# Earlier loads of the first weights, and a 128-token item turned in mid-chunk, in a fused attention, mixture-of-experts and SwiGLU kernel

## The chip, the cores and the metric

The kernel runs on one core of a Trainium2 chip. The metric is the device time of one execution, in microseconds (us); the median of three runs is given. TensorE is called PE here, VectorE DVE, ScalarE ACT, GpSimd POOL and SyncE SP, as the profile does.

## What is computed

Block-sparse attention (2 batches, 8 heads, 768 positions, 64 per head) gives 1536 tokens of 512 numbers. Each token goes to the one expert of eight that a gate picks, then through a dense SwiGLU layer. Cut to what matters:

```python
x = attention(q, k, v)                                   # 1536 x 512
logits = x @ w_gate + modality_bias[modality_id]
e_idx = np.argmax(logits, axis=1)
gate_w = softmax(logits)[arange(N), e_idx]
for e in range(8):
    mask = e_idx == e
    h = np.maximum(x[mask] @ w1[e], 0.0)                 # 512 -> 1024
    out[mask] = gate_w[mask, None] * (h @ w2[e])         # 1024 -> 512
x = out
return (silu(x @ w_g) * (x @ w_v)) @ w_o                 # 512 -> 1536 -> 512
```

## The kernel before

**Stages.** Attention runs over 24 units of 128 tokens and four heads (`st_s`, `st_e`, `st_t`, `st_v`). A finished block of 128 tokens is stored to the scratch tensor `x_d` (L728), turned (`st_x`, L349) and multiplied with the gate matrix (`st_l`, L360). Routing (`route`, `route_early`, `route_where`, `route_items`) builds index tables on DVE with small matmuls on PE. The experts' work is cut into items, `KIND = "TQQSP"`: item 0 has 384 tokens of the fullest expert, chosen from the first 768 tokens alone, items 1 and 2 have 512 tokens, item 3 has 128 and item 4 has 256. The SwiGLU layer follows.

**Two floats for one.** Every product is three matmuls (`mm3`, L820 to L822): high by high, low by high, high by low. So tokens and weights are split into a high part, which ACT writes, and a low part, which DVE writes: `xh` and `xl` of the tokens (L770, L771), `wh` and `wl` of a weight chunk (L801, L802), `hh` and `hl` of the hidden layer (L839, L842), `yh` and `yl` of the result (L874, L875).

**An item.** Its tokens are gathered from `x_d` into `xs` by indirect DMAs on POOL's queue (`gather`, L748, 128 rows each), scaled by the gate weight on DVE (`scale_x`, L755), and turned on PE with their split (`split_x`, L768 to L771; for the 128-token item `split_x1`, L792 to L794). For 384 tokens `split_x` has four parts of three transposes, which use the PSUM banks V, P, V, P in turn. There are two V banks and one P bank, so the fourth part waits until DVE has read the second. Then come four chunks of the hidden layer (`hidden`, 24 matmuls each, in two halves with a bank T each) and four chunks of the projection (`project`, 24 matmuls each), and `store_y` moves the result out of PSUM.

**Weights.** A chunk is 512 KB. SP reads the expert's number from the table `tab` into a register (L936) and issues the chunk's DMA into one of three `raw` buffers (`load_w`, L816). `load_to(n)` issues the loads up to the n-th, `split_to(n)` splits chunks up to the n-th and issues loads that far ahead that three are under way. The chunks' order is the list `preps`; `take` hands out a split chunk and has the one three places further split.

**What sets the order.** The program is written out in the order in which each engine is to work (a manual schedule); every engine runs its instructions in that order and waits on semaphores. Two places matter here.

The first is the change from attention to item 0, here the first seam. `route_early` finds the fullest expert (L450 writes `tab`), forms the index of its tokens, gathers them and then loads three chunks:

```python
first_x.append(gather(pl["xg"], *idx_of(0), rows=128 * b))    # L468
load_to(RB)                                                   # L469, RB = 3
```

Further down come the scaling (L1092), the split of the first chunk (L1094) and the split of the tokens (L1100), then item 0's hidden layer (L1115).

The second is the change from item 1's projection to item 2's hidden layer, here the second seam. Item 3's 128 tokens are scaled and turned between the two:

```python
    bg_step(STEPS["Q"])      # L1308, after each of four projected chunks
scale_x(xs)                  # L1318, after the fourth
x1 = split_of(3, xs)         # L1319
```

`bg_step` runs pieces of a list in the background: the decoding of the SwiGLU weights from 64-bit floats (L1237 to L1258) and the routing tables for the output rows. `sorted_tokens` (L1194 to L1200) is called after the third projected chunk: 24 small matmuls, and a copy of their result by DVE (L1200).

Of the kernel before, what the change touches and what calls it, by code (L numbers as in the profile page):

```python
# [7 lines left out]
F32 = mybir.dt.float32  # L8
# [4 lines left out]
ALU = mybir.AluOpType  # L13
# [6 lines left out]
def sparse_attention_moe_swiglu_kernel(  # L20
# [18 lines left out]
    nc = tc.nc  # L39
# [41 lines left out]
    NC1 = FF // 256  # L81
# [351 lines left out]
    def route_early():  # L433

        b = GROUPS[0][1]
        c0 = cnt[:, 0]
        TB_ = BLOCKS["T"]
        w = w_p.tile([128, 6, E], F32, tag="r_ew", bufs=1, name="r_ew")
        m8, fs, n0 = w[:, 0, 0:1], w[:, 0, 1:2], w[:, 0, 2:3]
        nc.vector.tensor_reduce(out=m8, in_=c0, op=ALU.max, axis=AX.X)  # L440
        yield
        nc.vector.scalar_tensor_tensor(out=w[:, 1], in0=c0, scalar=m8, in1=wts, op0=ALU.is_equal, op1=ALU.mult)
        nc.vector.tensor_scalar(out=n0, in0=m8, scalar1=-1.0, scalar2=float(-CT), op0=ALU.mult, op1=ALU.max)
        nc.vector.tensor_scalar(out=sc[0][:, 16:17], in0=m8, scalar1=float(CT), scalar2=None, op0=ALU.min)
        yield
        nc.vector.tensor_reduce(out=fs, in_=w[:, 1], op=ALU.max, axis=AX.X)
        yield
        nc.vector.scalar_tensor_tensor(out=w[:, 2, 0:TB_], in0=fs.to_broadcast([128, TB_]), scalar=-16.0,
                                       in1=kc[:, 0, 0:TB_], op0=ALU.mult, op1=ALU.add)
        nc.vector.tensor_scalar(out=tab[:, 0, 0:1], in0=fs, scalar1=-1.0, scalar2=float(E), op0=ALU.mult, op1=ALU.add)  # L450
        nc.vector.tensor_scalar(out=w[:, 3], in0=wts, scalar1=fs, scalar2=None, op0=ALU.is_equal)
        yield
        TB = [128, b, TB_]
        nc.vector.tensor_tensor(out=bo[:, 0:b, 0:TB_], in0=w[:, 2, 0:TB_].unsqueeze(1).to_broadcast(TB),
                                in1=code[:, 0:b].unsqueeze(2).to_broadcast(TB), op=ALU.is_equal)
        nc.vector.scalar_tensor_tensor(out=cnt[:, 2], in0=w[:, 3], scalar=n0, in1=c0, op0=ALU.mult, op1=ALU.add)
        nc.vector.tensor_scalar(out=w[:, 4:6].rearrange("p a e -> p (a e)")[:, 0:b], in0=fm_r[:, 0:b], scalar1=fs,
                                scalar2=-float(TB_), op0=ALU.is_equal, op1=ALU.mult)
        yield True
        ip = bank("T")  # L460
        for t in range(b):
            for j in range(2):
                nc.tensor.matmul(out=ip[:, 0:TB_], lhsT=a1[0, j][:, t, :], rhs=bo[:, t, 0:TB_],
                                 start=(t == 0 and j == 0), stop=(t == b - 1 and j == 1))
        nc.vector.tensor_copy(out=idx[:, 0:TB_], in_=ip[:, 0:TB_])
        nc.vector.tensor_tensor(out=code[:, 0:b], in0=code[:, 0:b],
                                in1=w[:, 4:6].rearrange("p a e -> p (a e)")[:, 0:b], op=ALU.add)
        first_x.append(gather(pl["xg"], *idx_of(0), rows=128 * b))  # L468
        load_to(RB)  # L469
        yield  # L470

    first_x = []
# [258 lines left out]
    pl = {}  # L731


    RB, WB = 3, 3
# [18 lines left out]
    def scale_x(xs):  # L753
        for t in xs:
            nc.vector.tensor_scalar(out=t[:, 0:DM], in0=t[:, 0:DM], scalar1=t[:, DM:DM + 1], scalar2=None, op0=ALU.mult)  # L755
# [38 lines left out]
        nc.vector.tensor_tensor(out=xl, in0=p, in1=xh.bitcast(F32), op=ALU.subtract)  # L794
        return xh, xl

    def split_w(pool, src, eng, tags=("wh", "wl")):
        a, b = src.shape[1], src.shape[2]
        wh = pool.tile([128, a, b], F32R, tag=tags[0], name="wh")
        wl = pool.tile([128, a, b], F32R, tag=tags[1], name="wl")  # L800
        nc.scalar.activation(out=wh, in_=src, func=ACTF.Copy)  # L801
        eng.tensor_tensor(out=wl, in0=src, in1=wh.bitcast(F32), op=ALU.subtract)  # L802
        return wh, wl

    def load_w(pool, e, which, c):
# [46 lines left out]
    def project(c, hs, w, yp, cols=(0, 1), between=None):  # L852
        for k in range(4):
            if k == 2 and between is not None:
                between()
            kk = 4 * (c % 2) + k
            h = hs[kk // 2]
            for dd in cols:
                sl = slice(128 * dd, 128 * dd + 128)
                own = len(yp) == 1 and len(cols) == 2  # L860
                y = yp[0][:, dd] if own else yp[dd][:, 0]
                mm3(y, w[0][:, k, sl], w[1][:, k, sl], h[0][:, kk % 2, :], h[1][:, kk % 2, :],
                    kk == 0 and (dd == 0 or not own), kk == 2 * NC1 - 1 and (dd == 1 or not own))
# [53 lines left out]
    for j in range(NS):  # L917
# [3 lines left out]
        if j == JS - 1:  # L921

            one = [(wn, JS, c) for c in range(NC1) for wn in ("w1", "rows")]
# [3 lines left out]
    ready = {}  # L927
# [4 lines left out]
    def load_to(n):  # L932
        while n_load[0] < min(n, len(preps)):
            wn, j, c = preps[n_load[0]]
            if j not in e_reg:
                e_reg[j] = nc.sync.value_load(tab[0:1, 0, j:j + 1], min_val=0, max_val=E - 1)  # L936
            loaded[wn, j, c] = load_w(pl["raw"], e_reg[j], wn, c)
            n_load[0] += 1

    def split_to(n, limit=None):  # L940
        limit = len(preps) if limit is None else limit
        while n_split[0] < min(n, limit):
            key = preps[n_split[0]]
            load_to(min(n_split[0] + RB, limit))
            ready[key] = split_w(pl["wc"], loaded.pop(key), nc.vector)
            n_split[0] += 1
        load_to(min(n_split[0] + RB, limit))

# [3 lines left out]
    def split_of(j, xs, tags="VP", later=None):  # L952
        if KIND[j] == "S":
            return split_x1(pl["s1"], xs)
        return split_x(pl["xg"], xs, tags, later)
# [135 lines left out]
    st_x(NT - 2)  # L1091
    scale_x(first_x[0])  # L1092
    st_v(NM - 1)
    split_to(1, 2 * NC1)  # L1094
    heads.close()
    open_h()

    while rg:
        adv(1000)
    x = split_of(0, first_x[0])  # L1100
    st_z(NT - 2)
    st_x(NT - 1)
    split_to(2, 2 * NC1)
# [176 lines left out]
    def take(*key):  # L1280
        split_to(done[0] + WB)
        done[0] += 1
        return ready.pop(key)
# [6 lines left out]
    bg += [decode(wn, 0, i, fw_p) for wn in "gvo" for i in range(2)]  # L1290
    load64()
    load64()
    hs, tok_rows = [], []
    for c in range(NC1):
        hs.append(hidden(c, x, take("w1", 1, c)))
        if c == 0:
# [5 lines left out]
    for c in range(NC1):  # L1302
        if c % 2 == 0:
            yp = y_banks(512, "T" if c else "S")
        project(c, hs, take("w2", 1, c), yp)
        if c % 2:
            store_y(c // 2, yp, bass.ds(sa, 512), bass.ds(sd, 512))
        bg_step(STEPS["Q"])  # L1308
        if c == 1:
            half = []  # L1310
            x = split_of(2, xs, later=half)
            xs = gather(pl["xg"], *idx_of(3))
        if c == 2:
            half.pop()()
            sorted_tokens(*tok_rows)
            rt_x.close()
            pl["s1"] = moe.enter_context(tc.tile_pool(name="s1", bufs=1, side="right", reuse_waits="tile"))
    scale_x(xs)  # L1318
    x1 = split_of(3, xs)  # L1319


    hs, h1, hb = [], [], []
# [197 lines left out]
```

## Time and profile before

| | |
|---|---|
| three runs | 587.97, 588.63 and 590.27 us, median 588.63 us |
| the profiled execution | 590.24 us |
| its span, first to last instruction | 588.3 us |
| PE busy | 567.2 us, 96% of the span, 3372 matmuls |
| PE weight loads | 475.9 us, 81% |
| DVE, ACT, POOL busy | 384.6, 211.5 and 67.3 us (65%, 36%, 11%) |
| mean granted TensorE clock | 0.990 of full speed |
| bytes by DMA | 64.83 MB, mean 110 GB/s |

The profile is of one execution. Its own time, 590.24 us, lies 1.94 us over its span. An engine's busy time counts overlapping instructions once. The granted clock is the share of TensorE's full clock of 2.4 GHz that the chip let through; 0.50 is its lower level, 1.2 GHz. A row of the timeline has the start in us from the span's start, the time from its first start to its last end, engine, line, operation, output and inputs, shape, and the count of merged instructions; brackets give the idle time before it and what ended it. Matmuls are pipelined, so the distance of starts tells their pace, and their own durations overlap.

### The profile page before, as it was taken

What the parts mean: (1) busy time and instruction counts of PE and PEld (TensorE: products, weight loads), DVE (VectorE), ACT (ScalarE), POOL (GpSimd) and SP (SyncE); (2) the same over time, 40 slices, a digit from 0 to 9 for tenths busy, and PEclk for the clock granted to TensorE, in tenths of its full rate; (3) what the DMA queues carried; (4) which work ended last, traced back from release to release, by engine and by line L of the source; (5) the groups of instructions that cost most, each with busy time, mean ns of one, the idle gap of its engine ahead of it and who ended that gap; (6) DMA issues with size and microseconds to landing.
All of it is one profiled execution on the core that took longest, in us unless ns stands there. A gap on an engine that the chain in (4) does not pass through costs nothing.

```text
span 588.3 us, 8858 instructions
## 1 busy us (share of the span) xinstructions
PE 567.2 (96%) x3372; PEld 475.9 (81%) x3372; DVE 384.6 (65%) x760; ACT 211.5 (36%) x370; POOL 67.3 (11%) x196
## 2 busy tenths in 40 slices
PE   7999997999999899999999999999999999999996
PEld 6879985999788688899788888888888888888884
DVE  5688797578978477685366577478648847853223
ACT  4687945442434254463233342121222211211110
POOL 5773012031301000000100000000000000000025
PEclk9999999799999899999999999999999999999999
DMA  9999348446635255562022232112203202200013
GB/s 245 227 241 208 96 92 257 114 127 201 200 117 180 87 176 165 173 197 77 2 72 72 72 108 72 36 47 96 72 1 108 76 32 72 72 0 1 1 72 143
DMA packets 76429, 64.83 MB, mean 110 GB/s; under 512 B 24340, under 2 KB 70432, under 8 KB 76192
## 3 DMA queue, kind: packets, MB, share of 16 engines
q1 hardware_dynamic: 74304, 57.41, 34.3%
q0 software_dynamic: 2080, 6.82, 3.4%
q8 instruction: 27, 0.44, 0.3%
q14 instruction: 18, 0.15, 0.1%
HBM read 57.88 MB, written 6.35 MB: 109 GB/s over the span
## 4 chain that ended last, share of the span: by engine, by line
PE 47%; issue 2%; POOL 2%; DVE 0%; POOLq 0%
PE ps_T L820 11%; PE ps_T L821 11%; PE ps_T L822 11%; PE ps_S L820 3%; PE ps_S L822 3%; PE ps_S L821 3%; POOL out_dram L1470 2%; PE ps_P L820 1%; PE ps_V L820 1%; PE ps_P L821 1%; PE ps_V L821 1%; PE ps_V L822 1%; PE ps_P L822 1%; DVE acc L1465 0%; POOL between L1468 0%
## 5 line engine op out<-in xcount | busy, mean ns | idle before, releaser
L1448 DVE TENSOR_TENSOR hv<-sg,ps_T 128x512 f32<-128x512 f32 x36 | 24.7, 686 | 69.5 <-PE ps_T L822 69.5
L802 DVE TENSOR_TENSOR wl<-raw,wh 128x1024 fp32r<-128x1024 f32 x40 | 48.8, 1222 | 18.4 <-ACT wh L801 17.7
L1450 ACT ACTIVATE fh<-hv 128x512 fp32r<-128x512 f32 x36 | 22.8, 632 | 104.3 <-DVE hv L1448 104.3
L820 PE MATMUL ps_T<-yh,gh 128*128 128x512 f32 x144 | 57.0, 396 | 0.9 <-ACTq L1384 0.9
L821 PE MATMUL ps_T<-yl,gh 128*128 128x512 f32 x144 | 56.9, 395 | 0.0
L820 PE MATMUL ps_T<-yh,vh 128*128 128x512 f32 x144 | 56.9, 395 | 0.0
L821 PE MATMUL ps_T<-yl,vh 128*128 128x512 f32 x144 | 56.9, 395 | 0.0
L822 PE MATMUL ps_T<-yh,vl 128*128 128x512 f32 x144 | 56.9, 395 | 0.0
L822 PE MATMUL ps_T<-yh,gl 128*128 128x512 f32 x144 | 56.9, 395 | 0.0
L801 ACT ACTIVATE wh<-raw 128x1024 fp32r<-128x1024 f32 x40 | 41.9, 1055 | 14.7 <-PE ps_S L821 7.9
L820 PE MATMUL ps_T<-xh,wh 128*128 128x512 f32 (+2 forms) x124 | 46.0, 371 | 0.3 <-DVE hl L842 0.3
L821 PE MATMUL ps_T<-xl,wh 128*128 128x512 f32 (+2 forms) x124 | 45.1, 364 | 0.0
L822 PE MATMUL ps_T<-xh,wl 128*128 128x512 f32 (+2 forms) x124 | 45.1, 364 | 0.0
L1470 POOL DMA_INDIRECT out_dram<-acc,tk x12 | 11.7, 975 | 289.0 <-DVE acc L1465 287.2
L1446 ACT ACTIVATE sg<-ps_T 128x512 f32<-128x512 f32 x36 | 21.3, 592 | 58.3 <-PE ps_T L822 58.3
L1452 DVE TENSOR_TENSOR fl<-hv,fh 128x512 fp32r<-128x512 f32 x36 | 24.9, 692 | 25.1 <-ACT fh L1450 25.1
L820 PEld LDWEIGHTS ps_T<-yh,gh 128*128 128x128 f32 x144 | 27.0, 188 | 7.5 <-ACTq L1384 1.0
L822 PEld LDWEIGHTS ps_T<-yh,vl 128*128 128x128 f32 x144 | 27.0, 188 | 6.6
L820 PEld LDWEIGHTS ps_T<-yh,vh 128*128 128x128 f32 x144 | 27.0, 188 | 6.6
L822 PEld LDWEIGHTS ps_T<-yh,gl 128*128 128x128 f32 x144 | 27.0, 188 | 6.6
L821 PEld LDWEIGHTS ps_T<-yl,vh 128*128 128x128 f32 x144 | 27.0, 188 | 6.6
L821 PEld LDWEIGHTS ps_T<-yl,gh 128*128 128x128 f32 x144 | 27.0, 188 | 6.5
(309 smaller groups left out, 1306.2 us busy)
## 6 DMA issues: line engine op xcount, KB each, us to landing
raw<-in_moe_w_dram SPq DMA_DIRECT2D x40, 512.0 KB, 3.5
r<-in_moe_w_gate_dram SPq DMA_DIRECT2D x12, 512.0 KB, 3.4
r<-in_moe_w_val_dram SPq DMA_DIRECT2D x12, 512.0 KB, 3.5
r<-in_moe_w_out_dram SPq DMA_DIRECT2D x12, 512.0 KB, 3.8
ve<-in_v_dram SPq DMA_DIRECT2D x20, 192.0 KB, 5.3
ld<-in_k_dram SPq DMA_DIRECT2D x12, 256.0 KB, 5.9
ld<-in_q_dram SPq DMA_DIRECT2D x12, 256.0 KB, 5.7
x_d<-x SPq DMA_DIRECT2D x12, 256.0 KB, 5.5
```

The lines of the kernel that those rows point to most:

```text
L801: nc.scalar.activation(out=wh, in_=src, func=ACTF.Copy)
L802: eng.tensor_tensor(out=wl, in0=src, in1=wh.bitcast(F32), op=ALU.subtract)
L820: nc.tensor.matmul(out=out_, lhsT=ah, rhs=bh, start=start, stop=False)
L821: nc.tensor.matmul(out=out_, lhsT=ah, rhs=bl, start=False, stop=False)
L822: nc.tensor.matmul(out=out_, lhsT=al, rhs=bh, start=False, stop=stop)
L1446: nc.scalar.activation(out=sg, in_=gp_, func=ACTF.Silu)
L1448: nc.vector.tensor_tensor(out=hv, in0=sg, in1=vp_, op=ALU.mult)
L1450: nc.scalar.activation(out=hh, in_=hv, func=ACTF.Copy)
L1452: nc.vector.tensor_tensor(out=hl, in0=hv, in1=hh.bitcast(F32), op=ALU.subtract)
L1470: st = nc.gpsimd.indirect_dma_start(out=out, in_=acc[n], in_offset=None, out_offset=bass.IndirectOffsetOnAxis(ap=tk[:, 0:1], axis=0))
```

## The change

Three edits.

`route_early` now loads two chunks as soon as the expert's number stands in `tab`, ahead of the index and the gather; the third chunk's load comes after the split of the first.

The low part of the first chunk is no longer made in one go with its high part. It is kept as a function (`later`) and called between the two halves of the tokens' split.

Item 3's tokens are scaled behind `sorted_tokens` after the third projected chunk, and turned by a call in the middle of the fourth, between its twelfth and thirteenth matmul.

```diff
@@ route_early
         nc.vector.tensor_scalar(out=w[:, 3], in0=wts, scalar1=fs, scalar2=None, op0=ALU.is_equal)
+        load_to(2)
         yield
...
         first_x.append(gather(pl["xg"], *idx_of(0), rows=128 * b))
-        load_to(RB)
         yield
@@ split_w
-    def split_w(pool, src, eng, tags=("wh", "wl")):
+    def split_w(pool, src, eng, tags=("wh", "wl"), later=None):
...
         nc.scalar.activation(out=wh, in_=src, func=ACTF.Copy)
-        eng.tensor_tensor(out=wl, in0=src, in1=wh.bitcast(F32), op=ALU.subtract)
+
+        def low():
+            eng.tensor_tensor(out=wl, in0=src, in1=wh.bitcast(F32), op=ALU.subtract)
+
+        if later is None:
+            low()
+        else:
+            later.append(low)
         return wh, wl
@@ split_to
-    def split_to(n, limit=None):
+    def split_to(n, limit=None, later=None):
...
-            ready[key] = split_w(pl["wc"], loaded.pop(key), nc.vector)
+            ready[key] = split_w(pl["wc"], loaded.pop(key), nc.vector, later=later)
@@ the first seam
-    split_to(1, 2 * NC1)
+    low = []
+    split_to(1, 2, low)
+    load_to(RB)
     heads.close()
     open_h()
...
-    x = split_of(0, first_x[0])
+    half = []
+    x = split_of(0, first_x[0], later=half)
+    low.pop()()
+    half.pop()()
     st_z(NT - 2)
@@ the second seam
-    hs, tok_rows = [], []
+    hs, tok_rows, one = [], [], []
...
-        project(c, hs, take("w2", 1, c), yp)
+        project(c, hs, take("w2", 1, c), yp, between=(lambda: one.append(split_of(3, xs))) if c == 3 else None)
...
             pl["s1"] = moe.enter_context(tc.tile_pool(name="s1", bufs=1, side="right", reuse_waits="tile"))
-    scale_x(xs)
-    x1 = split_of(3, xs)
+            scale_x(xs)
+    x1, = one
```

In the changed kernel the lines below L449 have other numbers: L802 becomes L804, L816 becomes L823, L820 to L822 become L827 to L829, L936 becomes L943.

SP's queue at the first seam, before, from the store of the gate weights on. `x_d` is the scratch tensor, `ve` are the values of the last attention block, `raw` is a weight chunk.

```order
L397 DMA x_d<-gate 128x6x1 [waits DMAHW1_49,DVE_49]
L728 DMA x_d<-x 128x512 [waits DMAHW2_49,DVE_49]
L156 DMA ve_185<-in_v_dram 96x8x64 [waits DMAHW3_49,PE_49]
L156 DMA ve_185<-in_v_dram 80x8x64 [waits DMAHW4_49,PE_49]
L936 TENSOR_LOAD tab [waits DVE_49]
L936 ISA x2
L816 ISA
L816 DMA raw<-in_moe_w_dram 128x4x256 [waits DMAHW5_49]
L816 ISA
L816 DMA raw<-in_moe_w_dram 128x4x256 [waits DMAHW6_49]
L816 ISA
L816 DMA raw<-in_moe_w_dram 128x4x256 [waits DMAHW7_49]
```

The same place after the change. The read of `tab` (now L943) stands right behind the store of the gate weights, and the rows go on from there:

```order
L823 DMA raw<-in_moe_w_dram 128x4x256 [waits DMAHW2_49]
L823 ISA
L823 DMA raw<-in_moe_w_dram 128x4x256 [waits DMAHW3_49]
L728 DMA x_d<-x 128x512 [waits DMAHW4_49,DVE_49]
L156 DMA ve_185<-in_v_dram 96x8x64 [waits DMAHW5_49,PE_49]
L156 DMA ve_185<-in_v_dram 80x8x64 [waits DMAHW6_49,PE_49]
L728 DMA x_d<-x 128x512 [waits DMAHW7_49,DVE_49]
L728 DMA x_d<-x 128x512 [waits DMAHW0_49,DVE_49]
L728 DMA x_d<-x 128x512 [waits DMAHW1_49,DVE_49]
L823 ISA
L823 DMA raw<-in_moe_w_dram 128x4x256 [waits DMAHW2_49]
```

Two loads moved ahead of one store and of both loads of `ve`; the third moved behind the last three stores of `x_d`.

DVE's queue at the first seam, before, from the last scaling of item 0's tokens on:

```order
L755 TENSOR_SCALAR xs<-xs 128x512 [waits DMASW2_49]
L720 TENSOR_SCALAR l<-ps_V 128x4 [waits PE_49]
L722 RECIPROCAL li<-l 128x4 [waits DVE_49]
L725 TENSOR_TENSOR x<-ps_V,li 128x256 [waits DVE_49]
L802 TENSOR_TENSOR wl<-raw,wh 128x1024 [waits DMAHW5_49,Activation_49]
L771 TENSOR_TENSOR xl<-ps_V,xh 128x384 [waits Activation_49]
L771 TENSOR_TENSOR xl<-ps_P,xh 128x384 [waits Activation_49]
```

The same after the change:

```order
L755 TENSOR_SCALAR xs<-xs 128x512 [waits DMASW2_49]
L720 TENSOR_SCALAR l<-ps_V 128x4 [waits PE_49]
L722 RECIPROCAL li<-l 128x4 [waits DVE_49]
L725 TENSOR_TENSOR x<-ps_V,li 128x256 [waits DVE_49]
L771 TENSOR_TENSOR xl<-ps_V,xh 128x384 [waits DMAHW5_49,Activation_49]
L771 TENSOR_TENSOR xl<-ps_P,xh 128x384 [waits Activation_49]
L804 TENSOR_TENSOR wl<-raw,wh 128x1024 [waits DMAHW2_49]
L771 TENSOR_TENSOR xl<-ps_V,xh 128x384 [waits Activation_49]
L771 TENSOR_TENSOR xl<-ps_P,xh 128x384 [waits Activation_49]
```

The chunk's low part moved behind the first two low parts of the tokens.

PE's queue at the second seam, before: the last matmul of item 1's projection (`hh,wl`), the turn of item 3's tokens, the first matmuls of item 2's hidden layer (`xh,wh`):

```order
L822 MATMUL ps_T<-hh,wl 128x512
L792 MATMUL ps_V<-ident,xs 128x128 [waits DMASW3_49,DVE_49]
L792 MATMUL ps_V<-ident,xs 128x128 x3
L820 MATMUL ps_T<-xh,wh 128x512 [waits Activation_49]
L821 MATMUL ps_T<-xl,wh 128x512
```

The turn after the change, in the middle of the projection's fourth chunk:

```order
L829 MATMUL ps_T<-hh,wl 128x512
L792 MATMUL ps_V<-ident,xs 128x128 [waits DMASW3_49,DVE_49]
L792 MATMUL ps_V<-ident,xs 128x128 x3
L827 MATMUL ps_T<-hh,wh 128x512
L828 MATMUL ps_T<-hl,wh 128x512
```

The four transposes moved up by twelve matmuls. At the old place item 2's hidden layer now follows the projection at once. Its first half waits only for a weight chunk's high part on ACT; its second half waits for the first of the two `yl` of `store_y`. On DVE the scaling moved from behind those two `yl` and two decoding steps (L1241, L1244) to right behind the copy L1200.

## Rows read from the trace of the kernel before

**Rows 1.** Page, busy time of each engine, its share and instructions.

```profile
PE 567.2 (96%) x3372; PEld 475.9 (81%) x3372; DVE 384.6 (65%) x760; ACT 211.5 (36%) x370; POOL 67.3 (11%) x196
```

**Rows 2.** PE's waits, the longest: in total, times, longest.

```profile
PE ps_V L792 <- DVE xs L755: 2.9, 1, 2.9
```

**Rows 3.** Stretches of 1 us: length, busy PE, PEld, DVE, ACT, POOL, clock, DMA share, GB/s.

```profile
87.00:88.00 1.00, 1.00 (x11) 1.00 (x11) 0.94 (x4) 0.28 (x1) 0.00 (x0) 1.00 0.00 0
...
99.00:100.00 1.00, 0.01 (x1) 0.00 (x0) 0.36 (x1) 0.19 (x1) 0.00 (x0) 1.00 1.08 387
...
102.00:103.00 1.00, 0.01 (x1) 0.01 (x1) 1.00 (x4) 0.06 (x1) 0.00 (x0) 0.64 0.45 168
```

**Rows 4.** Timeline of SP at the first seam.

```profile
91.08 1.59 SPq L816 DMA_DIRECT2D raw<-in_moe_w_dram  x3
92.77 8.45 SPq L728 DMA_DIRECT2D x_d<-x  x3
```

**Rows 5.** Timeline of POOL at the first seam, the third of three gathers.

```profile
92.37 0.95 POOL L748 DMA_INDIRECT xs<-x_d,idx  x1 [0.30 <-issue]
```

**Rows 6.** Timeline of DVE at the first seam.

```profile
85.67 0.15 DVE L450 TENSOR_SCALAR tab<-r_ew 128x1 int32<-128x1 f32 x1
...
97.76 0.87 DVE L755 TENSOR_SCALAR xs<-xs 128x512 f32<-128x512 f32 x2
99.64 0.48 DVE L755 TENSOR_SCALAR xs<-xs 128x512 f32<-128x512 f32 x1 [1.01 <-DMA xs<-x_d,idx]
...
100.79 1.22 DVE L802 TENSOR_TENSOR wl<-raw,wh 128x1024 fp32r<-128x1024 f32 x1
...
102.39 0.55 DVE L771 TENSOR_TENSOR xl<-ps_P,xh 128x384 fp32r<-128x384 f32 x1
```

**Rows 7.** Timeline of ACT at the first seam.

```profile
100.61 0.49 ACT L770 ACTIVATE xh<-ps_V 128x384 fp32r<-128x384 f32 x1 [1.42 <-PE ps_V L768]
...
106.49 1.99 ACT L801 ACTIVATE wh<-raw 128x1024 fp32r<-128x1024 f32 x2
```

**Rows 8.** Timeline of PE at the first seam.

```profile
102.99 0.90 PE L768 MATMUL ps_P<-ident,xs 128*128 128x128 f32 x3 [1.45 <-DVE xl L771]
...
105.55 0.67 PE L820 MATMUL ps_T<-xh,wh 128*128 128x384 f32 x1
...
109.18 0.34 PE L822 MATMUL ps_T<-xh,wl 128*128 128x384 f32 x1
109.35 0.34 PE L820 MATMUL ps_T<-xh,wh 128*128 128x384 f32 x1
```

**Rows 9.** Timeline of PE at the second seam.

```profile
191.30 0.39 PE L820 MATMUL ps_T<-hh,wh 128*128 128x512 f32 x1
...
193.79 0.39 PE L822 MATMUL ps_T<-hh,wl 128*128 128x512 f32 x1
...
197.46 0.48 PE L820 MATMUL ps_T<-xh,wh 128*128 128x512 f32 x1
...
201.42 0.39 PE L821 MATMUL ps_T<-xl,wh 128*128 128x512 f32 x1
```

**Rows 10.** Timeline of DVE at the second seam.

```profile
190.72 0.17 DVE L1200 CAST tok<-ps_T 128x12 int32<-128x12 f32 x1 [1.19 <-remote]
...
194.17 1.37 DVE L875 TENSOR_TENSOR yl<-ps_T,yh 128x512 f32 x2 [2.14 <-ACT yh L874]
...
196.51 0.48 DVE L755 TENSOR_SCALAR xs<-xs 128x512 f32<-128x512 f32 x1
```

**Rows 11.** Stretch of 1 us behind the second seam, columns as in rows 3.

```profile
198.00:199.00 1.00, 1.00 (x4) 0.72 (x4) 0.63 (x1) 1.00 (x2) 0.00 (x0) 0.50 0.06 16
```

**Rows 12.** Gathers after 120 us: shortest, median, longest ns; first and last start.

```profile
L748 POOL DMA_INDIRECT xs<-x_d,idx x11: 944/946/1723, 129.2 to 189.2; - x11
```

**Rows 13.** DMA issues, KB each, median us to landing; whole span, then 84 to 108 us.

```profile
raw<-in_moe_w_dram SPq DMA_DIRECT2D x40, 512.0 KB, 3.5
...
x_d<-x SPq DMA_DIRECT2D x4, 256.0 KB, 8.4
```

## The prediction

> **What bounds the kernel.** I read the busy times first: PE is busy for 96% of the span [rows 1]. Other engines' time is therefore worth only what it makes PE wait or slow down, and I looked for both. The list of PE's waits has 2.9 us at L792 as its longest [rows 2], at the second seam; the stretches of 1 us show a second place, around 100 us, where PE did almost nothing for a whole microsecond and the granted clock then fell in the middle of the next but two [rows 3]. The timelines of these two seams carry the rest. What the reader is to see: at both seams the clock stands at its lower level of 1.2 GHz behind the gap [rows 3, 11], and PE pays twice, once by waiting and once by slow matmuls.
>
> **First seam, what happens now.** The third gather of item 0's tokens goes out at 92.37 [rows 5], right behind three weight loads at 91.08 to 92.67 [rows 4]. Its tokens are scaled only at 99.64, after 1.01 us of waiting for that DMA, while the first two were scaled back to back from 97.76 [rows 6]. At that time the DMA engines are full (share 1.08, 387 GB/s); at 87 to 88 us they are empty [rows 3]. Then DVE makes the chunk's low part (100.79, 1.22 us) ahead of the tokens' low parts, although the first high part of the tokens was done at 100.61 + 0.49 = 101.10 [rows 6, 7]. The bank P comes free when the second low part ends at 102.94, and PE, which waited 1.45 us for it, turns the last part at 102.99 and starts the hidden layer at 105.55 [rows 6, 8].
>
> **Term 1, the earlier loads.** The expert's number is written at 85.82 [rows 6]. I estimate 1 to 2 us for the register and the issue, so the first two chunks (1 MB) go out by 88 and move while the engines are empty. At the 387 GB/s of the full stretch [rows 3], 1 MB takes 2.7 us. Beside the gather then remain the `ve` loads and the stores, and the third chunk follows the last store of `x_d`, whose issue ended at 101.22 [rows 4]. Without 1.5 MB beside it I expect the third gather to land before DVE's turn at 98.63, where the second scaling ends; then the scaling waits for nothing and what follows comes 1.0 us earlier. The bounds: 0, if the gather is slow for another reason, and 1.01 us, the wait itself; nothing below zero from this term, since less is in flight beside the gather. I take 1.0, because the wait is put down to that DMA and its stretch is the fullest. What SP is moved past: one store and the two `ve` loads are queued behind 1 MB now; the `ve` are for the last block, whose second unit's result DVE finishes only behind the scaling at 98 us, and a store took 8.4 us to land in this stretch at its fullest [rows 13]. What hides the delay is the empty time before 88 us; I cost it at nothing, and if that cover fails it is a wait of PE for `ve` of 1 or 2 us.
>
> **Term 2, the low part between the halves.** Before, the first low part of the tokens could have started at 101.15 and started when the chunk's ended, at 101.92 to 102.01: 0.8 us, which the bank P hands on to PE. The chunk's low part is now needed by the third matmul of the hidden layer, and ends near 102.2 by the same durations, before PE is there. Bounds 0 and 1.22 us; I take 0.8. PE would turn the last part at 102.99 - 1.8 = 101.2.
>
> **Term 3, the clock behind the first seam.** From 102.99 to 105.55 PE turned the last part, ran a gate product and turned a block at the lower clock: 2.56 us. At twice the clock that is between 1.3 and 2.56; I take 1.65, since the short matmuls do not halve. The hidden layer's first eleven matmuls took 109.18 - 105.55 = 3.63 us, and then 0.17 us each [rows 8], so 1.9 at full clock. If the clock stays up, 0.9 + 1.7 = 2.6 us come back. It may stay up: I estimate the waits that remain as 0.5 us before the third scaled tile and 0.7 at the bank P, where DVE's wait for the tile alone was 1.01 and PE's at the bank 1.45. Bounds 0 and 2.6; I take 2.6.
>
> **Term 4, the turn in mid-chunk.** Between the starts of the projection's last matmul and the hidden layer's first lie 3.67 us [rows 9]. Of these 0.23 are the matmul itself (eleven took 2.49 from 191.30), 2.9 the wait [rows 2], and some 0.45 the four transposes, which only move. PE waited because DVE scaled the tokens at 196.51, behind two `yl` and two decoding steps [rows 10]. Now the scaling follows the copy L1200, at 190.81 to 191.29, and PE reaches the turn at 191.30 [rows 9, 10]: they meet within 0.1 us. What is late next: item 2's hidden layer waits for nothing of `store_y` in its first half (2.8 us), and the first `yl`, done at 194.86 before [rows 10] and some 0.5 later now, is there for the second. DVE's chunk split behind the scaling comes 0.5 us later and is needed three chunks on. I take 2.9 saved less 0.1; bounds 0, if the whole wait moves into the chunk, and 2.9.
>
> **Term 5, the clock behind the second seam.** The ten matmuls from 197.46 took 3.96 us to 201.42 [rows 9], most of them at the lower clock [rows 11], against 10 x 0.23. With no gap there is no fall: 1.65 us; bounds 0 and 1.65.
>
> **Sum.** 1.0 + 0.8 + 2.6 + 2.8 + 1.65 = 8.85 us of the profiled execution's 590.24, so 581.4. The median of the runs, 588.63, lies 1.6 us under that execution. Part of the difference may be slow-clock time that other runs do not have and cannot get back; I split it and predict **580.6 us**. Edits to Python lists and closures cost nothing; no instruction is added. Behind the seams the work is PE's own for nearly all of the span [rows 1], so I see nothing that would give the time back later.
>
> **A rule against term 1.** POOL's third gather instruction took 0.95 us, and the eleven later ones between 0.944 and 1.723, median 0.946 [rows 5, 12], so POOL was not held up in making this one, though it can be. The Trainium skill, "SBUF — State Buffer", in its note on the "DVE blocks DMA" trap, says that a DMA issued by GpSimd looks slow when VectorE holds the port that GpSimd needs to write descriptors, and that the transfer itself is not short of bandwidth. By that rule the loads' place would not matter, term 1 would be zero, and the time would be that of the third rival; the row speaks against it, and the sum goes by the row.
>
> **Rivals.**
>
> 1. *The clock falls at the first seam all the same.* For: PE has waits of 0.5 and 0.7 us left there, between short transposes. Against: nothing as empty as 99 to 100 us remains. Term 3 then gives between 0 and 1: 590.24 - 6.25 to 7.25, less the 0.8 for the median, 582.2 to 583.2.
> 2. *The turn waits in mid-chunk.* The copy L1200 waited 1.19 us itself for a release that the profile cannot name [rows 10], and the scaling now stands behind it. Each microsecond that it slips stops PE in mid-chunk. With the old wait of 2.9 and a fall of the clock, terms 4 and 5 are gone: 590.24 - 4.4 - 0.8 = 585.0.
> 3. *The gather is late for another reason,* so the change does not do what the first edit says. Term 1 is zero, the gap before the third tile stays and the clock falls with it: only terms 2, 4 and 5, 5.25 us: 584.2.
> 4. *Slower: the third chunk arrives too late.* Its load now waits in SP's queue for the last store, about 100.3 us with term 1, where it was out by 92.67 [rows 4]. Its high part stands on ACT, and its low part on DVE, ahead of the first hidden chunk's `hh` and `hl`, which free the bank T for the second chunk. A load lands in 3.5 us at the median [rows 13], at 103.8; ACT made the two splits at 106.49 before [rows 7] and would come to this one near 104.4. Later than that, each microsecond stops PE, and the clock falls, for 2.6. Slower than now needs 8.85 - 2.6 = 6.25 us of stop, so a landing after 110.7, over 10 us after issue, longer than the 8.4 of the stores in the fullest stretch. At 13.5 us it would be 590.24 + 3.1 - 0.8 = 592.5.
>
> **Chances.** The forecast 0.60; rival 1 0.18; rival 2 0.07; rival 3 0.10; rival 4 0.03, and 0.02 for smaller gains than all of these. A measurement of this kernel tells about 0.5%, 2.9 us, from no change: faster means under 585.7. The forecast and rivals 1 and 3 lie there whole, rival 2 for the most part, so 0.88 faster, 0.10 the same, 0.02 slower. The range for 8 in 10 goes down by the unsplit 0.8 us and about 1 us of spread between runs, 578.6, and up over rivals 1 and 3 to 585.0.
>
> **What would show it.** In the changed profile: two `raw` issues near 87 us and no DMA wait ahead of the third scaling; the chunk's low part third among five on DVE; the hidden layer's first matmul near 102.8; no lower clock from 102 to 109 and from 198 to 201; item 3's transposes among the projection's matmuls, with under 0.3 us of wait, and item 2's first matmul right behind the last. The prediction is wrong if PE waits at L792 for over 1 us, if the third scaling still waits for its DMA, or if a wait for bank T appears before item 0's second hidden chunk.

## The result and the profile after

| kernel | median us | lowest to highest | executions | ratio to before, 95% interval |
|---|---|---|---|---|
| before, beside the change | 589.45 | 587.97 to 592.07 | 4 | |
| the change | 584.02 | 580.64 to 584.46 | 4 | 0.9885 [0.9858, 0.9912] |
| the change again (run e10) | 582.61 | 580.53 to 584.32 | 6 | 0.9870 [0.9842, 0.9898] |

The change is faster by 1.2 to 1.3%. The forecast of 580.6 against 588.63 is a ratio of 0.9864, inside both intervals, and 584.02 lies inside the range. But the median of the first four executions is 3.4 us above the forecast. Of the ten executions of the change three, with a mean granted clock of 0.999, took 580.53, 580.64 and 581.12 us; the other seven, with 0.986 to 0.996, took 582.45 to 584.46. The profiled one (584.02 us, span 582.3) has 0.986.

A mean clock does not say where the clock was low. In this profile it is low twice: at the first seam, as shown below, and from 9 to 16 us, in the attention, ahead of every edit. Stretches of 1 us, columns as in [rows 3]:

```profile
9.00:10.00 1.00, 0.00 (x0) 0.02 (x1) 0.97 (x4) 0.95 (x4) 0.27 (x2) 0.68 1.22 290
10.00:11.00 1.00, 0.99 (x5) 1.00 (x6) 0.16 (x1) 0.55 (x2) 0.00 (x0) 0.50 1.22 291
```

By the first seam nothing of that is left to see: the expert's number is written at 85.59 us, where it was 85.67 [rows 6].

The busy times and PE's waits of the change, from the page and the list of waits (in total, times, longest):

```profile
PE 564.0 (97%) x3372; PEld 473.8 (81%) x3372; DVE 385.5 (66%) x760; ACT 211.4 (36%) x370; POOL 67.3 (12%) x196
```

```profile
PE ps_S L687 <- ACT qz L645: 1.9, 2, 1.6
PE ps_V L768 <- DVE xs L755: 1.8, 2, 1.6
...
PE ps_P L768 <- DVE xl L771: 0.7, 1, 0.7
```

The wait at L792, the longest before [rows 2], is gone. That for the scaled tokens at the first seam is now among the two longest.

**Second seam.** Timeline of PE in the change (start, length, line, what it writes and reads, idle before):

```profile
189.74 0.60 PE L792 MATMUL ps_V<-ident,xs 128*128 128x128 f32 x4
190.09 0.48 PE L827 MATMUL ps_T<-hh,wh 128*128 128x512 f32 x1
...
192.72 0.39 PE L829 MATMUL ps_T<-hh,wl 128*128 128x512 f32 x1
192.95 0.40 PE L827 MATMUL ps_T<-xh,wh 128*128 128x512 f32 x1
...
195.28 0.39 PE L828 MATMUL ps_T<-xl,wh 128*128 128x512 f32 x1
```

The four transposes stand in the middle of the chunk, wait for nothing and cost 190.09 - 189.74 = 0.35 us. The hidden layer's first product starts 0.23 us behind the last of the projection, which was 3.67 [rows 9], and its eleventh at 195.28, where it was 201.42: 6.14 us earlier. Of these 1.56 come from ahead of the seam (the product at 190.09 answers to that at 191.30 [rows 9], with the 0.35 of transposes before it), so the second seam gave 4.58 us.

**First seam.** Timeline of the change there, all engines, the rows that answer to [rows 4 to 8]:

```profile
86.76 1.01 SPq L823 DMA_DIRECT2D raw<-in_moe_w_dram  x2
88.44 0.35 SPq L728 DMA_DIRECT2D x_d<-x  x1
88.88 0.96 SPq L156 DMA_DIRECT2D ve<-in_v_dram  x2
...
92.29 0.95 POOL L748 DMA_INDIRECT xs<-x_d,idx  x1 [0.31 <-issue]
...
96.54 0.48 DVE L755 TENSOR_SCALAR xs<-xs 128x512 f32<-128x512 f32 x1
...
98.53 0.88 DVE L755 TENSOR_SCALAR xs<-xs 128x512 f32<-128x512 f32 x2 [1.51 <-DMA xs<-x_d,idx]
...
99.07 0.72 PE L768 MATMUL ps_V<-ident,xs 128*128 128x128 f32 x2 [1.65 <-DVE xs L755]
...
101.35 1.22 DVE L804 TENSOR_TENSOR wl<-raw,wh 128x1024 fp32r<-128x1024 f32 x1
101.49 0.90 PE L768 MATMUL ps_P<-ident,xs 128*128 128x128 f32 x3 [0.67 <-DVE xl L771]
...
104.05 0.67 PE L827 MATMUL ps_T<-xh,wh 128*128 128x384 f32 x1
```

The loads went out at 86.76 as forecast, and the wait at the bank P fell from 1.45 to 0.67. But the scaling still waits for its DMA, now 1.51 us, and PE with it. It is the second tile that DVE waits for; the third is scaled right behind it, from 98.93 on. The stretches of 1 us (length, busy PE, PEld, DVE, ACT, POOL, clock, DMA share, GB/s) show what that does:

```profile
92.00:93.00 1.00, 1.00 (x20) 0.77 (x19) 0.76 (x3) 0.59 (x2) 0.71 (x1) 1.00 1.51 250
93.00:94.00 1.00, 1.00 (x24) 0.83 (x23) 0.74 (x3) 0.95 (x3) 0.24 (x1) 1.00 1.05 145
...
97.00:98.00 1.00, 0.30 (x1) 0.14 (x1) 0.02 (x1) 0.97 (x2) 0.00 (x0) 1.00 0.45 168
98.00:99.00 1.00, 0.00 (x0) 0.00 (x0) 0.47 (x2) 0.00 (x0) 0.00 (x0) 1.00 0.06 20
...
101.00:102.00 1.00, 0.51 (x3) 0.50 (x3) 1.00 (x2) 0.34 (x1) 0.00 (x0) 0.76 0.92 267
102.00:103.00 1.00, 1.00 (x16) 0.68 (x14) 1.00 (x3) 0.49 (x1) 0.00 (x0) 0.50 0.59 70
```

PE is empty for a whole microsecond, from 98 to 99, as it was from 99 to 100 before [rows 3], and the clock falls again between 101 and 102. Two more things are to be seen. At 92 to 94 us the DMA engines are full (shares 1.51 and 1.05) but move only 250 and 145 GB/s: that is when the `ve` loads of 88.88 run, in packets of 256 bytes (1283 of the 1308 packets in these 2 us are under 512 bytes). Before, they ran at 90 to 92 us (1119 of 1146 packets), as these stretches of the kernel before show:

```profile
90.00:91.00 1.00, 1.00 (x12) 0.99 (x10) 0.90 (x3) 0.27 (x1) 0.81 (x1) 1.00 0.57 149
91.00:92.00 1.00, 1.00 (x21) 0.81 (x19) 0.99 (x2) 0.87 (x2) 0.88 (x1) 1.00 0.81 184
```

And at 98 to 99 they are nearly empty while the gather's tail is still awaited.

### The profile page after: what moved, and what is told of

The parts are those of the page before. It is cut to its first block, busy times and chain, and to the rows that moved or that the text cites. A ratio compares the mean times of both kernels' runs of the same rounds, so it can differ in the third digit from the quotient of the medians.

```text
span 582.3 us, 8861 instructions
## 1 busy us (share of the span) xinstructions
PE 564.0 (97%) x3372; PEld 473.8 (81%) x3372; DVE 385.5 (66%) x760; ACT 211.4 (36%) x370; POOL 67.3 (12%) x196
## 4 chain that ended last, share of the span: by engine, by line
PE 48%; issue 2%; POOL 2%; POOLq 0%; DVE 0%
PE ps_T L827 11%; PE ps_T L829 11%; PE ps_T L828 11%; PE ps_S L827 3%; PE ps_S L829 3%; PE ps_S L828 3%; POOL out_dram L1482 2%; PE ps_P L827 1%; PE ps_V L827 1%; PE ps_V L828 1%; PE ps_P L828 1%; PE ps_V L829 1%; PE ps_P L829 1%; POOLq L1527 0%; POOL between L1480 0%
## 5 line engine op out<-in xcount | busy, mean ns | idle before, releaser
L804 DVE TENSOR_TENSOR wl<-raw,wh 128x1024 fp32r<-128x1024 f32 x40 | 48.8, 1222 | 18.1 <-ACT wh L801 17.4
L827 PE MATMUL ps_T<-yh,gh 128*128 128x512 f32 x144 | 57.0, 395 | 1.0 <-ACTq L1396 1.0
L829 PE MATMUL ps_T<-yh,vl 128*128 128x512 f32 x144 | 56.9, 395 | 0.0
L827 PE MATMUL ps_T<-yh,vh 128*128 128x512 f32 x144 | 56.9, 395 | 0.0
L829 PE MATMUL ps_T<-yh,gl 128*128 128x512 f32 x144 | 56.8, 395 | 0.0
L827 PE MATMUL ps_T<-xh,wh 128*128 128x512 f32 (+2 forms) x124 | 45.5, 367 | 0.3 <-DVE hl L849 0.3
L829 PE MATMUL ps_T<-xh,wl 128*128 128x512 f32 (+2 forms) x124 | 44.5, 359 | 0.0
L827 PEld LDWEIGHTS ps_T<-yh,gh 128*128 128x128 f32 x144 | 27.0, 187 | 7.7 <-ACTq L1396 1.2
L827 PEld LDWEIGHTS ps_T<-yh,vh 128*128 128x128 f32 x144 | 27.0, 187 | 6.6
L829 PEld LDWEIGHTS ps_T<-yh,gl 128*128 128x128 f32 x144 | 27.0, 187 | 6.6
L829 PEld LDWEIGHTS ps_T<-yh,vl 128*128 128x128 f32 x144 | 27.0, 187 | 6.6
```

What stands on the lines that cost most here:

```text
L827: nc.tensor.matmul(out=out_, lhsT=ah, rhs=bh, start=start, stop=False)
L829: nc.tensor.matmul(out=out_, lhsT=al, rhs=bh, start=False, stop=stop)
```

## The experiments

Theory after the change's first profile: the second seam gives its 4.5 us by itself; at the first the gather's tail is late because of what shares the DMA engines with it, the `ve` packets above all, and the clock falls because of PE's empty time there. Rivals: the clock falls whatever is done there; the gather is late for its own sake; the weights, not `ve`, are what matters. Runs e1 to e4 take the change apart, e5 to e8 and e11 add to it, e9 takes the loads back out of e5.

**e1, the second seam's edit alone.**

```diff
-        project(c, hs, take("w2", 1, c), yp)
+        project(c, hs, take("w2", 1, c), yp, between=(lambda: one.append(split_of(3, xs))) if c == 3 else None)
...
-    scale_x(xs)
-    x1 = split_of(3, xs)
+            scale_x(xs)
+    x1, = one
```

> The second seam's edit alone (terms 4 and 5), the first seam as in the kernel before. Theory: the two seams are independent, and this one is worth what the trace of the change showed there, 6.14 - 1.56 = 4.6 us: 584.8 against 589.4, no lower clock near 199 us, no wait at the turn. Rival: part of that came from the shift that the first seam gave (where decoding steps and loads meet the turn), so that alone it is worth under 3 us.

Measured: 586.07 us, ratio 0.9934 [0.9909, 0.9958], so 2.5 to 5.4 us less, 3.9 in the middle. No wait at L792, no lower clock from 195 to 201 us. The theory stands: this edit carries most of the change's gain and needs nothing of the first seam. The rival's "under 3 us" lies at the edge of the interval, but the profile shows no wait at the turn.

**e2, the earlier loads alone.**

```diff
+        load_to(2)
         yield
...
-        load_to(RB)
         yield
...
-    split_to(1, 2 * NC1)
+    split_to(1, 2)
+    load_to(RB)
```

> The earlier loads alone (term 1). Theory: the gather's tail is late for the ve loads and the stores that share its engines, not for the weights; the third gather lands 0.5 to 1.1 us earlier than before, the scaling still waits over 1 us, the chunk's low part still stands ahead of the tokens' low parts, and the clock falls: 0.3 to 1.1 us less than before, within what a measurement tells from no change. Rival (the forecast's term 1 with the clock): the third scaling does not wait and the clock stays: 2.5 us or more less.

Measured: 588.81 us, 0.9988 [0.9964, 1.0012], no difference that can be told. The third gather, issued at 91.22, was scaled at 97.97, after 1.19 and 0.17 us of waits for the DMA: 6.75 us behind its issue, where it was 99.64 - 92.37 = 7.27 before. PE still waited 1.45 us at the bank P, and the clock fell.

**e3, the low part between the halves alone.**

```diff
...
+    x = split_of(0, first_x[0], later=half)
+    low.pop()()
+    half.pop()()
```

> The low part between the halves alone (term 2), the loads as before. Theory: 0.8 us less at PE's last part of the tokens, 102.2 for 102.99, the emptiness at 99 to 100 us as before and the clock falls: 0.6 to 1.0 us less in all. Rival: PE's wait for the bank P was what dropped the clock; then the clock stays without the loads' edit and it is 2.5 us or more less.

Measured: 588.57 us, 0.9981 [0.9961, 1.0001], about 1.1 us less. DVE made the chunk's low part third of the five, and PE waited 0.53 us at the bank P in place of 1.45 [rows 8]. Rows of e3's timeline:

```profile
102.44 1.22 DVE L804 TENSOR_TENSOR wl<-raw,wh 128x1024 fp32r<-128x1024 f32 x1
...
102.58 0.90 PE L768 MATMUL ps_P<-ident,xs 128*128 128x128 f32 x3 [0.53 <-DVE xl L771]
```

The clock fell all the same, and it did so between 99 and 100 us (0.91 there, 0.50 behind), ahead of that wait: here that wait was not what dropped it.

**e4, both edits of the first seam.** The diffs of e2 and e3 together.

> Both edits of the first seam, the second as before. Theory: terms 1 and 2 add up with the clock falling in most executions: 1.2 to 1.6 us less, and executions in which the clock stays show about 3.4 us more. Rival: the first seam's edits are worth nothing by themselves (the 1.2 us by which PE came there earlier in the trace of the change came from a late release before the seam, not from them): 0 to 0.4 us less.

Measured: 588.4 us, 0.9979 [0.9956, 1.0003]: 1.2 us less, between -0.2 and 2.6. One execution of twelve had a mean clock of 0.995, and it was the shortest, 584.97 us. The rival is not excluded by the time alone; the row of e3 speaks for a real gain of under 1 us. Its expectation names a late release ahead of this seam; that is the last point under what was not expected.

The profiles of e2 and e4 tell one thing more on the second seam, which is unchanged in both. In both PE waits 2.87 us at L792. Behind it, at 198 to 199 us, e2 has the first row and e4 the second:

```profile
198.00:199.00 1.00, 1.00 (x6) 0.81 (x5) 0.40 (x1) 0.60 (x1) 0.00 (x0) 1.00 0.00 0
```

```profile
198.00:199.00 1.00, 1.00 (x4) 0.81 (x3) 0.93 (x1) 0.03 (x1) 0.00 (x0) 0.50 0.00 0
```

The same wait, and the clock at 1.00 in one and at 0.50, its level of 1.2 GHz, in the other.

**e5, the change with the last block's `ve` loads one block earlier,** into a buffer of the first batch, whose summary rows are loaded again. What is left beside the gather are the stores.

```diff
-        return ve[3 * (n // NBLK) + n % NBLK % 3]
+        return ve[2 if n == NT - 1 else 3 * (n // NBLK) + n % NBLK % 3]
...
+        if n == NT - 4:
+            return
         if n % NBLK + 3 < NBLK:
             ld_ve(n + 3)
+            if n == NT - 6:
+                for g in range(NG):
+                    nc.sync.dma_start(out=ve[2][WS:W, g, :, 0:D],
+                                      in_=vs_d[H * NSB:2 * H * NSB, :].rearrange("(h n) d -> n h d", h=H))
+            if n == NT - 5:
+                ld_ve(NT - 1)
```

> The changed kernel with the last block's two ve loads (352 KB in packets of 256 bytes) issued one block earlier, into another buffer, so that they do not run beside the gather. Theory: the gather's tail is late for what shares the DMA engines with it; without these packets the third gather lands 1 us or more earlier, the third scaling waits under 0.5 us and the clock stays up at the first seam: 580 to 581. Rival 1: the gather's end is set by its own packets or by the stores: the wait of about 1.5 us stays and the time with it, 584. Rival 2: the wait goes, but the clock falls all the same for the wait at the bank P: 582.5 to 583.5.

Measured: 581.0 us (579.74 to 583.85), 0.9856 [0.9828, 0.9885]. The three scalings run without a wait, and the clock stays at 1.00 from 97 to 106. Rows of e5's timeline:

```profile
96.89 1.27 DVE L755 TENSOR_SCALAR xs<-xs 128x512 f32<-128x512 f32 x3
...
100.25 0.55 PE L768 MATMUL ps_P<-ident,xs 128*128 128x128 f32 x3 [0.68 <-DVE xl L771]
...
101.70 0.42 PE L827 MATMUL ps_T<-xh,wh 128*128 128x384 f32 x1
```

The wait of 0.68 us at the bank P is still there, as in the change, and the clock does not fall for it. Five of the six executions have a mean clock of 0.995 or more; the profiled one, with 0.995, has its low stretch at 9 to 13 us. Its stretches at 92 and 93 us move 379 and 324 GB/s, where the change moved 250 and 145.

**e6, fill.** Transposes of a constant, that nothing reads, in PE's gaps.

```diff
+                if hold:
+                    warm(hold.pop(), "S")
...
+    warm(10, "S")
+    half = []
```

> The changed kernel with ten transposes of a constant on PE ahead of item 0's first turn and four ahead of the last part, so that PE is busy in the gaps while nothing else moves. They are extra work of PE with no use. Theory: the clock falls at the first seam because PE stands idle for 1.65 and 0.67 us; filled, it stays: 3.4 us less than the change, 580.6, although nothing arrives earlier. Rival: the clock falls for another reason, or the fill delays the turn: 584 to 585.

Measured: 582.33 us (581.8 to 582.84), 0.9873 [0.985, 0.9896]. The clock stays at 1.00 from 98 to 106 in the profile. Timeline of PE:

```profile
98.60 1.31 PE L184 MATMUL ps_S<-ident 128*128 128x128 f32 x10
99.75 0.72 PE L770 MATMUL ps_V<-ident,xs 128*128 128x128 f32 x3
...
101.33 0.60 PE L184 MATMUL ps_S<-ident 128*128 128x128 f32 x4
102.17 0.55 PE L770 MATMUL ps_P<-ident,xs 128*128 128x128 f32 x3 [0.24 <-DVE xl L773]
```

The fill costs PE time ahead of the first turn (the scaling of the first tile was done at 98.75, the turn starts at 99.75) and yet the worst of six executions is 582.84, below the change's 584.02. By the ratios no difference from the change can be told. The time came out 1.7 us above the theory's 580.6, though the clock did what the theory says.

**e7, fill with work that PE has to do anyway.**

```diff
+    st_z(NT - 2)
     half = []
     x = split_of(0, first_x[0], later=half)
     low.pop()()
+    st_x(NT - 1)
     half.pop()()
-    st_z(NT - 2)
-    st_x(NT - 1)
```

> The changed kernel with work that PE has to do anyway moved into the gaps: the gate product of the last block but one ahead of the first turn, and the last block's turn between the halves. Theory: both the gaps and the work behind them shrink: the hidden layer starts 0.8 to 1.5 us earlier even at the lower clock, and with the clock kept up 3.4 us more: 580 if the clock stays, 582.5 to 583.2 if it falls. Rival: the moved work delays DVE's or ACT's part of the split (one gate sum and one copy stand ahead), and nothing is gained: 584.

**e8, e7 and e5 together.**

> e7 and e5 together: the last block's ve loads earlier, and the gaps filled with work that has to be done. Theory: no gap over 0.5 us is left at the first seam, the clock stays in every execution: 579 to 580, the best of the four. Rival: the gather's wait is not from the ve loads; then it reads as e7.

Measured: e7 581.37 us (580.32 to 581.97), 0.9855 [0.9828, 0.9882]; e8 580.97 us (578.75 to 581.73), 0.9839 [0.981, 0.9868], the lowest of all. Both profiles keep the clock at the seam. By time e8 cannot be told from e7 or e5, and it missed its 579 to 580; the reason that its rival gives is refuted, as e8's three scalings wait for nothing although they start only 98.04 - 93.41 = 4.63 us behind the third gather's issue. What moving the work gains ahead of the first hidden product is given back behind it. PE waits there for the first chunk's low part, and ahead of the second chunk for the reader of a bank T, in e8 so:

```profile
102.53 0.44 PE L829 MATMUL ps_T<-xh,wl 128*128 128x384 f32 x1 [0.23 <-DVE wl L804]
...
107.62 0.44 PE L827 MATMUL ps_T<-xh,wh 128*128 128x384 f32 x1 [0.44 <-DVE hl L849]
```

At 136.22 it then waits 1.14 us for item 1's scaled tokens, where it waits 0.41 in e5.

**e9, e5 with the weight loads back behind the gather,** as before the change.

```diff
-        load_to(2)
...
         first_x.append(gather(pl["xg"], *idx_of(0), rows=128 * b))
+        load_to(RB)
...
```

> The changed kernel with the last block's ve loads one block earlier and the weight loads where they were before the change (three, behind the gather): is the first edit needed once the ve packets are out of the way? Theory A: the ve packets alone held the gather's tail; the third scaling waits under 0.5 us and the clock stays in most executions: 581 to 582. Theory B: the 1.5 MB of weights hold it as well; the third gather lands 6.5 us or more behind its issue, the scaling waits about 1 us or more, and the clock falls in most executions: 583.5 to 585.

Measured: 585.96 us, 0.9944 [0.9919, 0.9969]: theory B, 1 us above its range. Timeline of DVE, the third gather being issued at 93.20:

```profile
99.13 0.49 DVE L755 TENSOR_SCALAR xs<-xs 128x512 f32<-128x512 f32 x1 [0.83 <-DMA xs<-x_d,idx]
100.21 0.49 DVE L755 TENSOR_SCALAR xs<-xs 128x512 f32<-128x512 f32 x1 [0.60 <-DMA xs<-x_d,idx]
```

That is 7.01 us from issue to scaling, and the clock is at 0.50 from 101 on. Between e9 and e5 only the first edit differs, and the intervals do not meet: it is worth 5 us here (585.96 - 581.0), and nothing that can be told alone in e2.

**e10, the change again,** without an edit.

> The changed kernel itself once more, beside the other two, for its own spread: theory: most executions near 584 with a mean clock of 0.986 to 0.991, and one in four or fewer near 580.6 with 0.995 or more. Rival: the clock stays in half of them or more, and the median is 582 or less.

Measured: 582.61 us; two executions of six at 0.999, two at 0.995 and 0.996, two at 0.986 and 0.990. Between theory and rival; with the first four, three of ten have 0.999. In its profile the scaling waited only 0.29 and 0.16 us for the gather, and the clock was low at the seam for about half as long as in the first profile, from 103 to 107. Yet this execution, with a mean clock of 0.996, is the longest of the six, 584.32 us. PE waited 1.07 us for item 1's scaled tokens at 138.70, where it waited 0.16 in the first profile, and 2.5 us in place of 1.4 at one place of the attention (L334). So the seams and the clock are not all of the spread.

**e11, e8 with a free bank for the last part.**

```diff
-            p = bank(tags[j % 2])[:, 0:per * n].rearrange("p (k c) -> p k c", k=per)
+            p = bank(tags[j % len(tags)])[:, 0:per * n].rearrange("p (k c) -> p k c", k=per)
...
-    x = split_of(0, first_x[0], later=half)
+    x = split_of(0, first_x[0], "VPVS", half)
```

> e8 with the tokens' last part turned into a bank of the free pair S in place of P, so that PE does not wait 0.5 us for P's reader: a version to beat the others. Theory: the hidden layer's first product starts up to 0.5 us earlier, its third then waits for the chunk's low part by up to 0.5 us more: 580.5 to 581, 0 to 0.4 us under e8. Rival: the chunk's low part is the bound there: exactly e8's time, 581.

Measured: 581.61 us (580.12 to 583.25), 0.9866 [0.9839, 0.9892]. The rival: the wait moved from the bank to the chunk's low part, as this row of PE's waits in e11 shows.

```profile
PE ps_T L829 <- DVE wl L804: 1.0, 1, 1.0
```

The profiled execution has a mean clock of 0.999 and is the shortest of six, 580.12 us; four of the others have 0.986 to 0.991. So the "stays" of e11 in the table below holds for that one execution.

The first seam of the profiled executions, from the timelines (us); the clock's column says whether a lower clock stands between 99 and 110:

| kernel | loads early | `ve` early | third gather issued | first scaling | its waits for the DMA | first hidden product | first scaling to first product | clock |
|---|---|---|---|---|---|---|---|---|
| before | no | no | 92.37 | 97.76 | 1.01 | 105.55 | 7.79 | falls |
| e1 | no | no | 92.20 | 96.45 | 2.10 | 105.41 | 8.96 | falls |
| e3 | no | no | 92.34 | 96.60 | 2.19 | 105.14 | 8.54 | falls |
| e9 | no | yes | 93.20 | 97.82 | 1.43 | 105.44 | 7.62 | falls |
| e2 | yes | no | 91.22 | 95.65 | 1.36 | 103.88 | 8.23 | falls |
| e4 | yes | no | 93.64 | 98.05 | 1.25 | 105.64 | 7.59 | falls |
| the change | yes | no | 92.29 | 96.54 | 1.51 | 104.05 | 7.51 | falls |
| e10 | yes | no | 92.87 | 98.26 | 0.45 | 104.09 | 5.83 | falls |
| e6, fill | yes | no | 92.87 | 98.27 | 0.31 | 103.63 | 5.36 | stays |
| e7, work | yes | no | 91.59 | 96.98 | 0.32 | 101.05 | 4.07 | stays |
| e5 | yes | yes | 91.50 | 96.89 | 0 | 101.70 | 4.81 | stays |
| e8 | yes | yes | 93.41 | 98.04 | 0 | 101.70 | 3.66 | stays |
| e11 | yes | yes | 92.50 | 97.11 | 0 | 100.24 | 3.13 | stays |

## Why the prediction was right, and where it was not

**Faster, and the range: right.** The sum was 8.85 us of one execution; the profiled execution of the change is 590.24 - 584.02 = 6.2 us shorter, and the three executions with a mean clock of 0.999 come within 0.6 us of the forecast of 580.6. Term by term the profiles give 99.64 - 98.93 = 0.71 us from the third scaled tile, 0.78 at the bank P, nothing from the clock at the first seam and 4.58 at the second seam, together 6.07. What is missing is in the main term 3, 2.6 us. One sum of the chances is off: the 0.88 for faster leaves rival 2 out whole, though the sentence counts it for the most part.

**Term 1, the earlier loads (1.0 forecast): the step failed.** "Without 1.5 MB beside it I expect the third gather to land before DVE's turn at 98.63." The loads went out where I said, but the gather gained only 0.5 to 0.7 us: the third tile is scaled 7.0 to 7.4 us behind its issue in before, e1, e3 and e9, and 6.6 to 6.8 in the change, e2, e4, e7 and e10. The second, the one that DVE waits for in the change, gained nothing: where DVE waits for it, it is scaled 6.8 to 7.5 us behind its issue in e1, e3 and e9, and 7.2 to 7.5 in the change, e2, e4, e6 and e10.

What held them is what I named and costed at nothing, the `ve` loads queued behind 1 MB: "What hides the delay is the empty time before 88 us; I cost it at nothing". The price that I set on a failure of this cover, a wait of PE for `ve`, did not come; the gather paid. In the change the DMA engines move 10 GB/s from 87 to 88 us, so the 1 MB runs from 88 on, and the `ve` packets run 2 us later than before, at a time when the gathers' ran before: from 92 to 94 us the gathers' queue has 80 packets before the change and 11 in it. With the `ve` loads gone too the third tile is there in 5.4 us or less (e8). For the wait to go the loads' edit and e5's are both needed; e9 and e2 show that neither does it alone. The Trainium skill, "DMA: Bandwidth & Descriptors", Specifications, asks for 512 bytes or more in a transfer for the full rate; the trace agrees, with 145 and 250 GB/s at full engines while the 256-byte packets ran. And "DVE's turn at 98.63" was the time of one execution: in the change DVE came 1.2 us earlier, and met the gather's tail again.

**The rule against term 1: the row was right to outweigh it.** The note on the "DVE blocks DMA" trap in the Trainium skill's "SBUF — State Buffer" would have made the loads' place indifferent. Moving other transfers away did change when the gather landed, with POOL's third instruction at 0.95 us in before, e5 and e9 alike.

**Term 2, the low part (0.8 forecast): right.** The wait at the bank fell by 0.78 (change) and 0.92 (e3).

**Term 3, the clock at the first seam (2.6 forecast): failed in the profile, and was too small where the clock stayed.** It hung on "nothing as empty as 99 to 100 us remains"; with term 1 short, 98 to 99 was empty. This is rival 1, by the cause of rival 3. Where the clock stays it is worth somewhat more than I wrote. From the last part's start to the first product: 2.56 us in the change, 1.45 in e5. From the first product to the fourteenth: 4.31 (to 108.36) and 2.35 (to 104.05). Together 3.07 us.

**Term 4 (2.8) and term 5 (1.65): right, 4.58 for 4.45 in the profiles.** Term 4 is firm: the wait of 2.87 us stands in before, e2, e3 and e4 and in none with the edit. Term 5 is not: of these four profiles only before and e4 have the lower clock behind that wait. I costed one execution's fall as if every execution had it; by the medians, e1 is worth 3.9 us, between the two.

**Rivals 2 and 4** did not come. The turn waited for nothing in mid-chunk, and PE never waited for the bank T because of the third chunk.

**Do the terms add?** e1 and e4 give 3.9 + 1.2 = 5.1 us by their ratios, the change 6.8 and 7.7 by its own two. The intervals allow equality; a clock that stays only when all gaps are small would make the whole more than its parts, as e5 against e2 and e9 shows.

**A better version.** e8 is the lowest at 580.97, but its interval touches that of e5, e7, e11 and of the change. The profiles tell more if the attention is left out: from the write of the expert's number to the end of the span they take 496.7 us (the change), 496.4 (e10), 493.9 (e6), 493.8 (e7), 493.5 (e5), 493.5 (e8) and 492.8 (e11). So the clock kept at the seam goes with about 3 us less, and early `ve` loads, useless fill and owed work all do that. That owed work is worth more than the fill, or that it adds to the early `ve` loads, is not shown.

## What to carry to other kernels

Price a gather by everything on the DMA engines between its issue and its use, and by the rate of the packets, not by bytes alone: here 352 KB in 256-byte packets decided it as much as 1.5 MB of weights. A gap of PE costs its length each time and a lower clock only sometimes, so count the clock's part as a chance unless several executions show it. A load moved ahead in a queue pushes back what stands behind it, here 256-byte loads by 2 us, so ask what that will then run beside. And an edit that shows nothing alone may be the condition of the next one.

## What the runs showed that I had not expected

- **A fall of the clock is not fixed by the gap.** The same wait of 2.87 us ended with the clock at 1.00 in e2 and at 0.50 in e4. At the first seam it mostly went by the gaps: in the seven profiles in which PE waited 0.97 us or more in one piece for the scaled tokens it fell, in the five with the gaps filled or gone it stayed. In e10 it fell behind waits of 0.43, 0.32 and 0.68 us; in e5 it stayed behind one of 0.68 alone, and in e11 behind one of 0.98 for the chunk's low part. Each of these is one profiled execution.
- **The gather's tail comes from nearly empty engines:** a share of 0.06 at 98 to 99 us in the change, at 20 GB/s. Of the 11 packets that the trace has there two are of the gathers' queue; why those came last was not tried.
- **The attention's end has two timings, whatever the edit.** DVE's first scaling comes 5.4 us behind the third gather's issue in before, e5, e6, e7 and e10, and 4.25 to 4.63 in the others. This moves the wait for the gather by 1 us from one execution to the next. The expectation of e4 called it a late release; no run tested its cause.
